# A fused delta-rule and feed-forward kernel whose opening stage is put in an order of its own: K loaded first, norms by a root on VectorE, weights decoded by three engines

## Chip, cores and metric

The kernel runs on one core of a Trainium2 chip. The metric is the time of one execution on the device in microseconds (us), as the median of several runs. The executions of the kernel before lie between 822 and 830 us over all chips used here.

## The reference, cut to what matters

```python
k_n = k / (np.linalg.norm(k, axis=-1, keepdims=True) + 1e-06)       # (4, 8, 768, 48)
for t in range(S):                                                 # S = 768
    y[:, :, t] = np.einsum('bhd,bhde->bhe', q[:, :, t], state)
    v_old = np.einsum('bhde,bhd->bhe', state, k_n[:, :, t])
    state = state + b[t] * outer(k_n[:, :, t], v[:, :, t] - v_old)
x = y.transpose(0, 2, 1, 3).reshape(3072, 384)
h = x @ w_in                                                       # 384 x 2048
out = (0.5 * h * (1 + erf(h / sqrt(2)))) @ w_out                   # 2048 x 384
```

The weights `w_in` and `w_out` arrive as float64. The kernel takes the 64 bits as two 32-bit words and builds float32 values from them; this is the "decode".

## The kernel before

The sequence is cut into 12 chunks of 64 steps. For two chunks together (a "group") a 32x32 triangular system per head is inverted on VectorE by sixty dependent operations (the "elimination"), carried over to the other half by small matmuls (the "joins"), and then each chunk has its state steps. The feed-forward of chunk c runs beside the state steps of chunk c+1. A scheduler arranges the instructions of each engine by the priorities that the program text gives.

The decode of one tile of 512 (w_in) or 384 (w_out) columns, where `hi` and `lo` are the two words, each with a stride of two:

```python
nc.vector.tensor_scalar(e, hi, 20, 0x7FF, op0=ALU.logical_shift_right, op1=ALU.bitwise_and)
nc.vector.tensor_scalar(bits, hi, 0xFFFFF, 0x100000, op0=ALU.bitwise_and, op1=ALU.bitwise_or)
nc.gpsimd.tensor_scalar(e, e, 1151.0, 896.0, op0=ALU.min, op1=ALU.max)
nc.gpsimd.tensor_scalar(e, e, -896.0, float(2 ** 23), op0=ALU.add, op1=ALU.mult)
nc.vector.scalar_tensor_tensor(e, hi, 0x80000000, e, ALU.bitwise_and, ALU.bitwise_or)
nc.vector.scalar_tensor_tensor(dst, lo, 2.0 ** -32, bits, ALU.mult, ALU.add)
nc.vector.scalar_tensor_tensor(dst, dst, 2.0 ** -20, e.bitcast(F32), ALU.mult, ALU.mult)
```

And the order of the opening:

```python
interleave(gram_steps(0) + gram_steps(1) + v_steps(0) + inverse_steps(0),
           [(1.0, decode, n) for n in range(6)])
interleave(state_steps(0), gram_steps(2) + v_steps(1), [(1.0, decode, n) for n in range(6, n_in)])
for c in range(1, NC):
    ...   # c == 1: state(1), gram(3), inverse(1), feed-forward 0 and the rest of the decodes
```

Of the kernel before, what the change touches and what calls it, by code (L numbers as in the profile page):

```python
# [8 lines left out]
F32 = mybir.dt.float32  # L9
# [7 lines left out]
def kernel(  # L17
# [68 lines left out]
    def fetch_in(dst, src, u):  # L86
        rows = slice(u.c * C, (u.c + 1) * C)
        for p in range(2):
            nc.sync.dma_start(out=dst[HALF[p]],  # L89
                              in_=src[2 * u.a + p, :, rows, :].rearrange("h t d -> t h d"))  # L90

    def load(c):
        if c >= NC:
            return
        for a in range(NA):
            u = tiles[c, a] = Unit()
            u.c, u.a, u.n = c, a, c * NA + a
            u.t = (c % 2) * NA + a
            u.Kp, u.Qp = Kp[u.n % NKS], Qp[u.n % NQS]
            fetch_in(u.Kp[:, :, 0:D], k, u)  # L100
            fetch_in(u.Qp[:, :, 0:D], q, u)
# [8 lines left out]
    w_out_sb = cpool.tile([128, NF, DM], F32)  # L110
    bt = w_in_sb[0:B * H, 0, 0:2 * S].rearrange("n (c p t) -> n c p t", p=2, t=C)
# [3 lines left out]
    load(0)  # L115
    load(1)
# [3 lines left out]
    make_identity(nc, ident)  # L120
    mask = cpool.tile([128, C], F32)
    nc.gpsimd.memset(mask, 1.0)
    for p in range(2):
        nc.gpsimd.affine_select(out=mask[HALF[p]], in_=mask[HALF[p]], compare_op=ALU.is_ge,
                                fill=0.0, base=-1, pattern=[[1, C]], channel_multiplier=-1)
# [3 lines left out]
    for i in range(NKS):  # L129
        nc.gpsimd.memset(Kp[i][:, :, D:], 0.0)  # L130
    St = cpool.tile([128, NA, 2, NP, D], F32)
    nc.vector.memset(St, 0.0)
    low = cpool.tile([128, HB, HB], F32)
    nc.gpsimd.memset(low, 1.0)
    nc.gpsimd.affine_select(out=low, in_=low, compare_op=ALU.is_ge, fill=0.0, base=-1,
                            pattern=[[1, HB], [-1, HB]], channel_multiplier=0)
    Zf = [cpool.tile([128, NU, C], F32, name=f"Zf{i}") for i in range(2)]
    for i in range(2):
        nc.gpsimd.memset(Zf[i], 0.0)
# [3 lines left out]
    psB = sq("psB", NC, B * H)  # L143
    for c in range(NC):
        nc.tensor.transpose(psB[:, c, :], bt[:, c].rearrange("n p t -> n (p t)"),
                            ident[0:B * H, 0:B * H])
    for p in range(2):
        src = psB[HALF[p]].rearrange("q c (a p h) -> q c a p h", p=2, h=H)[:, :, :, p, :]
        nc.vector.tensor_scalar_mul(beta_m[HALF[p]], src, -1.0)
# [3 lines left out]
    w_parts = [(w_in_sb[:, m, f:f + WC], moe_w_in[m * 128:(m + 1) * 128, f:f + WC])  # L153
               for f in range(0, DF, WC) for m in range(NM)]
    w_parts += [(w_out_sb[:, f, :], moe_w_out[f * 128:(f + 1) * 128, :]) for f in range(NF)]
    w_raw = {}
    n_in = len(w_parts) - NF
# [3 lines left out]
    NS = NF * DM // (2 * WC)  # L161

    def fetch(n):
        if n >= len(w_parts):
            return
        src = w_parts[n][1]
        if n < n_in:
            w_raw[n] = stage[:, n % NS]
        else:
            w_raw[n] = su.tile([128, DM, 2], U32, tag="w_raw", name="w_raw")  # L170
        nc.sync.dma_start(out=w_raw[n].rearrange("q n w -> q (n w)"), in_=src.bitcast(U32))

    def decode(n):

        if n >= n_in - 1:
            fetch(n + 1)
        dst = w_parts[n][0]
        bits = dst.bitcast(U32)
        w = dst.shape[1]
        raw = w_raw.pop(n)  # L180
        lo, hi = raw[:, :, 0], raw[:, :, 1]
        e = su.tile([128, WC], U32, tag="w_e", name="w_e")[:, 0:w]
        nc.vector.tensor_scalar(e, hi, 20, 0x7FF, op0=ALU.logical_shift_right,  # L183
                                op1=ALU.bitwise_and)
        nc.vector.tensor_scalar(bits, hi, 0xFFFFF, 0x100000, op0=ALU.bitwise_and,
                                op1=ALU.bitwise_or)
        nc.gpsimd.tensor_scalar(e, e, 1151.0, 896.0, op0=ALU.min, op1=ALU.max)  # L187
        nc.gpsimd.tensor_scalar(e, e, -896.0, float(2 ** 23), op0=ALU.add, op1=ALU.mult)
        nc.vector.scalar_tensor_tensor(e, hi, 0x80000000, e, ALU.bitwise_and, ALU.bitwise_or)  # L189
        nc.vector.scalar_tensor_tensor(dst, lo, 2.0 ** -32, bits, ALU.mult, ALU.add)  # L190
        nc.vector.scalar_tensor_tensor(dst, dst, 2.0 ** -20, e.bitcast(F32), ALU.mult, ALU.mult)
        if n + NS < n_in:
            fetch(n + NS)

# [7 lines left out]

    def prep(c):
        us = [tiles[c, a] for a in range(NA)]
        g = c // 2
        if c % 2 == 0:
            gms[g] = wk.tile([128, 2 * NA, H], F32, tag="gm", name="gm")
        gm = gms[g][:, us[0].t:us[0].t + NA]
        n = ns[c] = wk.tile([128, NA, H], F32, tag="n", name="n", bufs=4)
        for u in us:  # L210
            kd = u.Kp[:, :, 0:D]
            ksq = wk.tile([128, H, D], F32, tag="ksq", name="ksq")
            nc.gpsimd.tensor_tensor(ksq, kd, kd, op=ALU.mult)  # L213
            nc.vector.tensor_reduce(n[:, u.a], ksq, axis=AX.X, op=ALU.add)  # L214
        flat = n.rearrange("q a h -> q (a h)")
        nc.gpsimd.tensor_tensor(flat, flat, half, op=ALU.pow)
        nc.vector.tensor_scalar_add(n, n, 1e-6)
        r = wk.tile([128, NA, H], F32, tag="r", name="r")
        nc.vector.reciprocal(r, n)
        nc.vector.tensor_tensor(gm, beta_m[:, c], r, op=ALU.mult)  # L220
        nc.vector.tensor_tensor(gm, gm, r, op=ALU.mult)
        if c == 0:
            nc.vector.tensor_scalar_mul(g_p, gm, -1.0)
# [5 lines left out]
    def transposed(u):  # L229
        u.KQt = wk.tile([128, NP, 2, 2, C], F32, tag="KQt", name="KQt", bufs=6)  # L230
        for x, src in ((0, u.Kp), (1, u.Qp)):
            psT = sq("psT", NP, 128)
            flat = src.rearrange("q h d -> q (h d)")
            for j in range(NP):
                nc.tensor.transpose(psT[:, j, :], flat[:, j * 128:(j + 1) * 128], ident)  # L235
            nc.scalar.copy(u.KQt[:, :, :, x, :], psT.rearrange("q j (p n) -> q j p n", p=2))  # L236

    def grams(u):
        g = u.c // 2
        if u.t == 0:  # L240
            Ds[g] = wk.tile([128, NU, HB], F32, tag="diag", name="diag", bufs=1)
            Os[g] = wk.tile([128, NU, HB], F32, tag="off", name="off", bufs=1)
        u.P = wk.tile([128, H, C], F32, tag="P", name="P", bufs=6)
# [7 lines left out]
        G = wk.tile([128, NP, 2, 2 * C], F32, tag="G", name="G", bufs=1)  # L251
        for r in range(2):
            nc.scalar.copy(G[:, :, r, :], psG[:, r])  # L253
        G = G.rearrange("q j r n -> q (j r) n")
        span = slice(u.t * H, (u.t + 1) * H)
        nc.scalar.copy(Ds[g][:, span], G[:, :, 0:HB])
        for p in range(2):
            lower = slice(p * C + HB, (p + 1) * C)
            nc.scalar.copy(Ds[g][lower, span], G[lower, :, HB:C])
        nc.vector.tensor_tensor(Os[g][:, span], G[:, :, HB:C],  # L260
                                gms[g][:, u.t].unsqueeze(2).to_broadcast([128, H, HB]),
                                op=ALU.mult)
        nc.gpsimd.tensor_tensor(u.P, G[:, :, C:], mask_h, op=ALU.mult)  # L263

    def eliminate_steps(g):
        steps = []

        def flip():
            Nus[g] = wk.tile([128, HB, HB], F32, tag="Nu", name="Nu", bufs=1)
# [4 lines left out]
                                    op=ALU.mult)  # L274
            nc.vector.transpose(Nus[g], Ds[g].rearrange("q u n -> q n u"))
            nc.vector.tensor_tensor(Nus[g], Nus[g], gl, op=ALU.mult)
# [26 lines left out]
        steps = [(3.0, flip)]  # L303
# [31 lines left out]
    def gram_steps(c):  # L335
# [3 lines left out]
        return [(1.0, prep, c)] + [(1.0, fn, u) for fn in (transposed, grams) for u in us]  # L339
# [129 lines left out]
    def ffn_steps(c):  # L469
        steps = [(1.3, fc1, c, f) for f in range(NF)]  # L470
        return steps + [(2.7, fc2, tiles[c, a], f, f + 4)
                        for a in range(NA) for f in range(0, NF, 4)]
# [12 lines left out]

    load_v(0)
    for n in range(NS):
        fetch(n)
    interleave(gram_steps(0) + gram_steps(1) + v_steps(0) + inverse_steps(0),
               [(1.0, decode, n) for n in range(6)])  # L490
    load(2)
    load_v(1)
    interleave(state_steps(0), gram_steps(2) + v_steps(1), [(1.0, decode, n) for n in range(6, n_in)])
    for c in range(1, NC):
# [3 lines left out]
        more = gram_steps(c + 2) + v_steps(c + 1) + (inverse_steps(c // 2 + 1) if c % 2 else [])  # L498
        if c == 1:
            interleave(state_steps(c), more, ffn_steps(c - 1),  # L500
                       [(1.0, decode, n) for n in range(n_in, NW)] + [(1.4 * NF, None)])
            start.close()
        else:
            interleave(state_steps(c), more, ffn_steps(c - 1))
# [31 lines left out]
```

## Time and profile before

| | before |
|---|---|
| time, median of the runs beside the change | 826.2 us (823.5 to 829.0) |
| profiled execution | 825.5 us |
| first feed-forward matmul (chunk 0) | 126.5 us |
| second feed-forward (chunk 1) | 213.1 us |
| third feed-forward (chunk 2) | 267.6 us |
| TensorE busy after 213 us | 598.6 of 612 us |

From the second feed-forward on, TensorE has no room, so the time is decided by when the feed-forwards can start. The starts come from the timeline of TensorE (the 1st and 97th matmul into psH).

### The profile page before, as it was taken

How to read it: one execution, taken by the hardware profiler on the slowest of the kernel's cores; microseconds unless marked ns; L12 is line 12 of the kernel's file. 1: busy time of each engine (PE TensorE's matmuls, PEld its weight loads, DVE VectorE, ACT ScalarE, POOL GpSimd, SP SyncE). 2: the span in 40 equal slices, each digit the busy share in tenths (PEclk: the TensorE clock that was granted, in tenths of full speed). 3: DMA queues.
4: the chain of work that ended last, by engine and by line, in shares of the span. 5: the costliest groups of instructions: out<-in, count | busy, mean ns of one | idle time of the engine just before them, and what ended most of it. 6: DMA issues, size and time to landing. Idle time of an engine off the chain costs nothing.

```text
span 825.5 us, 18581 instructions
## 1 busy us (share of the span) xinstructions
PE 707.5 (86%) x8148; PEld 515.3 (62%) x8148; DVE 376.1 (46%) x874; ACT 220.4 (27%) x510; POOL 190.9 (23%) x178
## 2 busy tenths in 40 slices
PE   4111078967999999999989999989999999999997
PEld 4100066735776865866857867757768668677684
DVE  3597997896012594031791023971125931202000
ACT  4200054201331512332403324213325122021120
POOL 8735357413002303013202014012023000000000
PEclk8555558887899999999999999999999999999999
DMA  7266034401101201203101102011011000000000
GB/s 173 111 154 107 19 90 106 102 33 30 35 16 29 50 1 30 40 12 61 19 20 31 30 21 54 6 30 31 2 30 30 2 21 2 10 11 1 20 1 19
DMA packets 84784, 32.85 MB, mean 40 GB/s; under 512 B 78048, under 2 KB 81120, under 8 KB 84704
## 3 DMA queue, kind: packets, MB, share of 16 engines
q1 hardware_dynamic: 80064, 26.75, 14.7%
q10 hardware_dynamic: 4640, 4.92, 2.4%
q8 instruction: 64, 1.05, 0.5%
q14 instruction: 16, 0.13, 0.0%
HBM read 26.94 MB, written 4.72 MB: 38 GB/s over the span
## 4 chain that ended last, share of the span: by engine, by line
PE 67%; DVE 20%; POOL 5%; issue 3%; SPq 2%; ACT 1%; DMA 1%; POOLq 0%; DVEq 0%
PE psO L460 28%; PE psH L451 25%; DVE tmp L283 4%; DVE Nu L285 4%; POOL w_e L187 2%; DVE w_e L189 2%; PE psT L235 2%; PE psS L426 2%; PE psG L248 2%; SPq L89 2%; PE psK L365 2%; PE psJ L320 1%; PE psJ L323 1%; DVE U L391 1%; PE psU L385 1%
## 5 line engine op out<-in xcount | busy, mean ns | idle before, releaser
L451 PE MATMUL psH<-xT,w_in_sb 128*128 128x256 f32 x1152 | 273.8, 390 | 4.0 <-ACT g L454 3.3
L460 PE MATMUL psO<-w_out_sb,g 128*128 128x384 f32 x768 | 273.6, 506 | 0.0
L451 PEld LDWEIGHTS psH<-xT,w_in_sb 128*128 128x128 f32 x1152 | 214.6, 192 | 36.4 <-ACT g L454 3.7
L460 PEld LDWEIGHTS psO<-w_out_sb,g 128*128 128x128 f32 x768 | 143.8, 194 | 91.0 <-issue 7.3
L454 ACT ACTIVATE g<-psH 128x256 f32<-128x256 f32 x192 | 73.7, 384 | 180.5 <-PE psH L451 179.9
L391 DVE TENSOR_TENSOR U<-psU,gm 64x192 f32<-64x192 f32 x88 | 31.2, 354 | 108.4 <-PE psU L385 107.5
L283 DVE TENSOR_TENSOR tmp<-Nu 128x30 f32<-128x30 f32 (+9 forms) x180 | 63.2, 351 | 4.6
L285 DVE TENSOR_TENSOR Nu<-Nu,tmp 128x30 f32<-128x30 f32 (+9 forms) x180 | 63.3, 352 | 4.4
L263 POOL TENSOR_TENSOR P<-G,mask 128x512 f32<-128x512 f32 x24 | 35.4, 1477 | 103.9 <-ACT G L253 103.9
L464 ACT COPY o_sb<-psO 128x384 f32<-128x384 f32 x24 | 11.5, 479 | 152.4 <-PE psO L460 152.4
L320 PE MATMUL psJ<-XM,off 32*32 32x32 f32 x768 | 16.4, 203 | 40.3 <-DVE XM L294 40.3
L235 PE MATMUL psT<-ident,Kp 128*128 128x128 f32 x96 | 17.0, 307 | 39.1 <-DMA Kp<-in_k_dram 29.1
L418 DVE TENSOR_TENSOR x<-psY,y 64x192 f32<-64x192 f32 x88 | 31.0, 352 | 38.4 <-PE psY L410 24.4
L320 PEld LDWEIGHTS psJ<-XM,off 32*32 32x32 f32 x768 | 15.2, 119 | 46.7 <-issue 43.4
L301 POOL MEMSET Zf<- 32x1024 f32 x12 | 11.4, 954 | 140.4 <-DVE Zf L298 140.1
L213 POOL TENSOR_TENSOR ksq<-Kp 128x384 f32<-128x384 f32 x24 | 20.7, 864 | 90.3 <-DMA Kp<-in_k_dram 90.0
L375 DVE TENSOR_TENSOR W<-psK,V 128x384 f32<-128x384 f32 x22 | 12.3, 557 | 61.9 <-PE psK L365 61.6
L187 POOL TENSOR_SCALAR w_e<-w_e 128x384 uint32<-128x384 uint32 (+1 forms) x28 | 27.4, 977 | 55.2 <-DVE w_e L183 54.9
L329 ACT COPY XM<-psJ 32x512 f32<-32x512 f32 x24 | 13.9, 578 | 97.7 <-PE psJ L320 97.6
L235 PEld LDWEIGHTS psT<-ident,Kp 128*128 128x128 f32 x96 | 12.7, 157 | 41.9 <-issue 35.9
L236 ACT COPY KQt<-psT 128x512 f32<-128x512 f32 x48 | 26.7, 588 | 43.6 <-PE psT L235 39.5
L214 DVE TENSOR_REDUCE n<-ksq 128x8 f32<-128x384 f32 x24 | 13.2, 552 | 55.2 <-POOL ksq L213 55.2
(75 smaller groups left out, 669.9 us busy)
## 6 DMA issues: line engine op xcount, KB each, us to landing
w_out_sb<-in_moe_w_in_dram SPq DMA_DIRECT2D x12, 512.0 KB, 4.7
w_raw<-in_moe_w_out_dram SPq DMA_DIRECT2D x16, 384.0 KB, 3.3
Kp<-in_k_dram SPq DMA_DIRECT2D x48, 96.0 KB, 2.9
Qp<-in_q_dram SPq DMA_DIRECT2D x48, 96.0 KB, 3.0
V<-in_v_dram SPq DMA_DIRECT2D x48, 96.0 KB, 2.9
out_dram<-o_sb ACTq DMA_DIRECT2D x48, 96.0 KB, 2.2
w_in_sb<-in_beta_dram ACTq DMA_DIRECT2D x2, 96.0 KB, 3.4
```

The source lines that it names most:

```text
L187: nc.gpsimd.tensor_scalar(e, e, 1151.0, 896.0, op0=ALU.min, op1=ALU.max)
L235: nc.tensor.transpose(psT[:, j, :], flat[:, j * 128:(j + 1) * 128], ident)
L236: nc.scalar.copy(u.KQt[:, :, :, x, :], psT.rearrange("q j (p n) -> q j p n", p=2))
L263: nc.gpsimd.tensor_tensor(u.P, G[:, :, C:], mask_h, op=ALU.mult)
L283: nc.vector.tensor_tensor(tmp, nu[:, j + 1:, j:j + 1].to_broadcast([128, n, j]), nu[:, j:j + 1, 0:j].to_broadcast([128, n, j]), op=ALU.mult)
L285: nc.vector.tensor_tensor(nu[:, j + 1:, 0:j], nu[:, j + 1:, 0:j], tmp, op=ALU.add)
L320: nc.tensor.matmul(psJ[low, 0, col], lhsT=off[top, u, :], rhs=xm[top, u, :], start=True, stop=True)
L391: nc.vector.tensor_tensor(pairs(u.U[HALF[p]], s), pairs(psU[HALF[p ^ s], p], s), pairs(gv[HALF[p]], s), op=ALU.mult)
L418: nc.vector.tensor_tensor(dst, src, pairs(u.y[HALF[p ^ s]], s), op=ALU.add)
L451: nc.tensor.matmul(psH, lhsT=w_in_sb[:, m, f * 128:(f + 1) * 128], rhs=xTs[c][:, m, :], start=(m == 0), stop=(m == NM - 1))
L454: nc.scalar.activation(gs[f], psH, ACT.Gelu)
L460: nc.tensor.matmul(u.psO, lhsT=gs[f][:, u.a * 128:(u.a + 1) * 128], rhs=w_out_sb[:, f, :], start=(f == 0), stop=(f == NF - 1))
```

## The change

Its intent: do nothing in the opening but what the first feed-forward needs, and decode the weights beside that feed-forward, with the work split over VectorE, ScalarE and GpSimd. The diff, cut to its core:

```diff
+    for u in first:                                    # K of four units first, halves on two queues
+        fetch_in(u.Kp[:, :, 0:D], k, u, (nc.sync, nc.scalar))
     ...                                                # then beta on the ScalarE queue, then Q
+    cuts = [0, WC // 2] + list(range(WC, DF + 1, WC))  # first 512 columns of w_in as two 256s
@@ decode
-        nc.gpsimd.tensor_scalar(e, e, 1151.0, 896.0, op0=ALU.min, op1=ALU.max)
-        nc.gpsimd.tensor_scalar(e, e, -896.0, float(2 ** 23), op0=ALU.add, op1=ALU.mult)
+        nc.scalar.activation(e, e, ACT.Relu, bias=lim[:, 0:1], scale=-1.0)
+        nc.scalar.activation(e, e, ACT.Relu, bias=lim[:, 1:2], scale=-float(2 ** 23))
+        nc.gpsimd.tensor_scalar(lo.bitcast(F32), lo, 2.0 ** -52, None, op0=ALU.mult)
+        nc.scalar.mul(dst, bits, 2.0 ** -20)
+        nc.gpsimd.tensor_tensor(dst, dst, lo.bitcast(F32), op=ALU.add)
+    def signed(n):                                     # one tile later
         nc.vector.scalar_tensor_tensor(e, hi, 0x80000000, e, ALU.bitwise_and, ALU.bitwise_or)
-        nc.vector.scalar_tensor_tensor(dst, lo, 2.0 ** -32, bits, ALU.mult, ALU.add)
-        nc.vector.scalar_tensor_tensor(dst, dst, 2.0 ** -20, e.bitcast(F32), ALU.mult, ALU.mult)
+        nc.gpsimd.tensor_tensor(dst, dst, e.bitcast(F32), op=ALU.mult)
@@ order
+    by_hand.enter_context(tc.manual_schedule(engines={DVE, Pool, Activation, PE}))
     ...   # squares; transposes, beta, products; root on VectorE; pack; flip; split
+    for step in steps:                                 # the elimination, nothing beside it
+        if step[1] not in (join, None): step[1](*step[2:])
+    for _, fn, n in decode_steps(0, NM): fn(n)         # three 256-column tiles
     ...   # joins of chunk 0; V scaling
+    interleave(state_steps(0), decode_steps(NM, 2 * NM))
     ...   # joins of chunk 1
+    by_hand.close()
+    early = gram_steps(2) + v_steps(1) + state_steps(1) + gram_steps(3) + v_steps(2)
+    late = inverse_steps(1)
+    interleave(ffn_steps(0), [(s_[0] * scale, *s_[1:]) for s_ in early] + late,
+               codes + [(0.8 * sum(s_[0] for s_ in codes), None)])   # all other decodes
```

## The prediction

> **What bounds the kernel now.** I read the page first, then the table of busy time by stretch, then the timeline of VectorE and GpSimd in two short windows. From the page, the 40 slices (20.6 us each):
>
> ```profile
> PE   4111078967999999999989999989999999999997
> DVE  3597997896012594031791023971125931202000
> POOL 8735357413002303013202014012023000000000
> PEclk8555558887899999999999999999999999999999
> ```
>
> TensorE is busy without a break from slice 11 on. Before that it is nearly empty for 100 us and VectorE is full. So there are two regimes, and the change touches the first alone. The border is the first matmul of the second chunk's feed-forward, at 213 us (timeline of TensorE). The table by stretch, cut at the events I found in that timeline (flip of the first group 33, first join 102, first feed-forward matmul 126.5, last weight decoded 173.5, second feed-forward 213):
>
> ```profile
> core 0: us, PE busy (x) PEld busy (x) DVE busy (x) ACT busy (x) POOL busy (x), PEclk, DMA share, GB/s
> 0.00:33.00 33.00, 13.76 (x172) 11.14 (x172) 10.52 (x27) 14.81 (x29) 26.29 (x33) 0.74 0.64 161
> 33.00:102.00 69.00, 4.35 (x16) 2.86 (x16) 60.84 (x138) 2.34 (x4) 33.19 (x33) 0.50 0.41 91
> 102.00:126.50 24.50, 19.46 (x541) 17.48 (x541) 23.29 (x39) 12.66 (x29) 12.69 (x16) 0.50 0.36 93
> 126.50:173.50 47.00, 39.47 (x365) 29.64 (x362) 39.50 (x86) 14.79 (x35) 25.77 (x27) 0.90 0.37 97
> 173.50:213.00 39.50, 31.87 (x438) 20.66 (x438) 26.86 (x66) 5.28 (x10) 6.80 (x6) 0.75 0.08 17
> 213.00:825.00 612.00, 598.58 (x6629) 433.50 (x6622) 215.08 (x524) 170.54 (x404) 86.13 (x65) 0.99 0.11 22
> ```
>
> After 213 us TensorE is 98% busy: those 612 us stay whatever the opening does. What can be won lies in the first 213 us, of which the second row is the emptiest for TensorE: 69 us in which the elimination of the first group and the decoding of twelve input weight tiles and the first output tile share VectorE.
>
> VectorE and GpSimd both look partly free in that table, but in the timeline they hold each other up. VectorE first, then GpSimd, over the same microseconds:
>
> ```profile
> 139.60 1.42 DVE L185 TENSOR_SCALAR w_out_sb<-w_raw 128x384 uint32<-128x384 uint32 x1
> 143.17 1.62 DVE L189 SCALAR_TENSOR_TENSOR w_e<-w_raw,w_e 128x384 uint32<-128x384 uint32 x1 [0.41 <-POOL w_e L188]
> 144.82 0.56 DVE L191 SCALAR_TENSOR_TENSOR w_out_sb<-w_out_sb,w_e 128x384 f32<-128x384 f32 x1
> 145.30 0.35 DVE L183 TENSOR_SCALAR w_e<-w_raw 128x384 uint32<-128x384 uint32 x1
> ```
>
> ```profile
> 139.22 1.58 POOL L263 TENSOR_TENSOR P<-G,mask 128x512 f32<-128x512 f32 x1
> 143.11 1.27 POOL L263 TENSOR_TENSOR P<-G,mask 128x512 f32<-128x512 f32 x1
> ```
>
> An operation of 0.35 us took 1.42 and ended 0.2 us after GpSimd's; one of 0.56 took 1.62 and ended 0.4 us after. I laid the intervals of VectorE's tensor_scalar, scalar_tensor_tensor and SBUF-only tensor_tensor instructions and of GpSimd's operations that read SBUF over each other: one or the other runs in 127 of the 140 us from 33 to 173. The two engines together are one resource here, 91% full. That, not VectorE's own share, is the bound of the opening.
>
> **What the Trainium skill says.** "SBUF — State Buffer", section "Who interferes with whom": VectorE and GpSimd share one port pair as an exclusive lock; a VectorE instruction with two SBUF inputs, or in a two-port mode (tensor_scalar can be), blocks against GpSimd reads; ScalarE waits for nobody. The two fences agree (1.42 against 0.35 us). "GPSIMD Engine Reference", section "Elementwise — side-by-side cycle accounting": a two-input operation on GpSimd takes 1.96 times VectorE's time at 2048 elements. The trace has 0.83 us for 128x384 (V, L226) against VectorE's 0.55 for a two-input operation of that size (L191): 1.5 times. "ScalarE: Activation LUTs", section "Table sets: the hidden batching unit": relu and copy are in every set, so the new Relu beside Gelu should cost no table loads. The kernel before has two loads of 1.28 us, with copies beside Gelu; it has no Relu. "DMA: Bandwidth & Descriptors", section "Issuing engines are not separate DMA queues": a second queue saves issue time only. Before, each K or Q issue took SyncE 0.63 us, 16 of them 10.2 us, so issue time is what the first 12 us hang on.
>
> **The change part by part.** Durations are start to start where nothing waited, from the timeline and the groups by form.
>
> *Until the first flip (31.2 us before).* K goes first, on two queues; all four pairs of inputs should still land only by 11 to 13 us, since 16 loads run on the same DMA engines and each transpose pair waits for its Q too. Then four products, each 2.0 us at half clock, and the copies of G (0.59 us, no longer through one buffer, whose waits cost ACT 3.5 and 3.8 us). The pow on GpSimd (2.9 us, twice) becomes 11 small VectorE operations near 0.2 us, off this path. Last pack about 1 us. Flip at 19.5 us: 11.5 us earlier.
>
> *Elimination alone.* The sixty operations without a wait: fifteen sizes from 0.19 to 0.41 us sum to 4.97, four times each 19.9, with gaps near 0.03 some 21.7 us. Around it the flip (1.95+1.25) and three transposes back (2.0+1.8+1.8): 30.5 us. GpSimd now makes off and P of four units beside it (0.6+1.4 each, 8 us), which hold the same port: I add 6. End at 19.5+30.5+6 = 56 us, against 105.6.
>
> *To the first feed-forward.* Three quarter-megabyte tiles are decoded ahead of the joins' copies in ScalarE's order (4 us), a join of half a group is 2x1.9 at half clock plus copies 2x1.2 (6 us, part overlapped), the first state took 17.5 us before and should take 12 to 14 with less on VectorE, and the second pair of joins sits ahead of the feed-forward on TensorE (some of 5 us). 56+23 = 79 us, against 126.5. This is the visible gain: 47 us.
>
> *What is given back.* By 126.5 the kernel before had decoded 17 of 28 tiles; the new one has three full-tile equivalents by 79. Left are nine of 512 columns and sixteen of 384. Per tile of 512: VectorE 0.34+0.34+0.60 = 1.28; GpSimd one tensor_scalar 0.70 and two two-input operations of 1.07 (0.79 for 384, scaled) = 2.84; together 4.1 us of the port (before: VectorE 2.5, GpSimd 1.25, 3.75). Per tile of 384: 1.01+2.17 = 3.2 (before 2.9). ScalarE takes three operations of 0.5 to 0.6, about 40 us in all, where it is free. So **the decode is taken off VectorE but not off the port**: 9x4.1+16x3.2 = 88 us. Beside it two chunks' gram work (P 4x1.47, pow 2x2.9, ksq 4x0.82, off and norms 3: 18 us) and V scaling (3.3): 109 us. My sums of single durations overstate the occupied time: for before up to 213 us the same bookkeeping gives 183 where the overlaid intervals give 166, so 0.91. Decoding is then over at the earliest at 79+0.91x109 = 178 us. The second group's elimination (25 us of port, 23 scaled) is ranked in the later half but fills gaps: between nothing and all of it comes ahead, 178 to 201. I take half, 189, and 1 to 3 us for the last matmuls: second feed-forward at 190 to 191.
>
> TensorE is not the bound in that stretch: the first feed-forward is 96x0.22+64x0.32 = 42 us plus about 23 for grams, state and joins, 65 us of 110.
>
> *Sum.* 190.5 + (823.6 - 213) = 801 us; 802 is recorded.
>
> **The rivals.** (a) *The port takes everything back*: the scheduler puts the second group's joins ahead of the second feed-forward in TensorE's order, and they wait until the whole elimination is through. All port work then ends near 201, transposes back and joins add 8 to 12: second feed-forward at 209 to 213, total 820 to 824. For it: before, TensorE waited 7.6 us for U and 4.3 for XM in this way. Against: the wait for XM was short, and there are 41 us of feed-forward to fill in. (b) *The port is not what it seems*: with GpSimd's operations long and VectorE's few, and ScalarE in between, VectorE's PSUM work and stream transposes (3x1.9 us a group) overlap GpSimd and the port is fully used; decoding ends near 170, total near 780. Against: 91% was used already. (c) *The opening hides TensorE's clock*: with TensorE 60% busy from 79 on it may stay at half clock (0.50 in the second and third rows), and 65 us become 100, near the decode's length; 5 to 10 us worse.
>
> **Range and chances.** Between (b) and (a) with (c): 780 to 826, 802 in the middle; 8 in 10 within 782 to 822. The 2% border is 807, so a second feed-forward later than 196 makes it "same". The half taken of the elimination decides it: faster 0.62, same 0.35, slower 0.03. Slower needs the decode past 225 us, which only a bad order of instructions would do.
>
> **What would show it.** In the new profile: the first flip near 19 and back-transposes ended near 56; first feed-forward matmul near 79; last output tile finished near 180 to 195; second feed-forward near 190, and 611 us from there to the end. GpSimd's busy time up from 191 to over 240, VectorE's down by 30 to 45, ScalarE's up by about 45, still two table loads. VectorE's scalar_tensor_tensor in the decode should show means well above 0.55 for 384 columns, ended by GpSimd. Wrong: if the decoding ends by 165 the port was not the limit; if TensorE waits more than 10 us at the joins of the second group it is rival (a); if the first feed-forward starts after 95, the hand-set order stalls and my chain there is wrong.

## The result, and the profile after

The change is slower: 857.6 us (855.6 to 859.1) against 826.2, ratio 1.038 with a 95% interval of 1.033 to 1.043. My range ended at 822.

| | before | predicted | after |
|---|---|---|---|
| first flip of the elimination | 31.2 | 19.5 | 27.6 |
| elimination and its transposes over | 105.6 | 56 | 72.8 |
| first feed-forward | 126.5 | 79 | 105.0 |
| last weight tile decoded | 175.3 | 189 | 219.6 |
| second feed-forward | 213.1 | 190.5 | 225.9 |
| third feed-forward | 267.6 | (245) | 299.4 |
| profiled end | 825.5 | 802 | 853.8 |

From the third feed-forward on the two are alike (558 us before, 554 after). Everything that was lost was lost earlier: 13 us until the second feed-forward and 19 between the second and the third. In all sixteen kernels it takes 554 to 560 us from the third feed-forward to the end, but 612 to 634 from the second. So the start of the third feed-forward, not of the second, tells the time. The page's slices of the kernel after (21.3 us each):

```profile
PE   4101565658779999999999999999999989999998
DVE  4486457767941259402297122693033960201100
POOL 2925988799111140301501202303014000000000
PEclk9655576788859999999999999999999999999999
```

GpSimd (POOL) is now the busiest engine of slices 5 to 10, mostly with eights and nines. Busy time by stretch, in the columns of the prediction's table (PE, PEld, DVE, ACT, POOL, clock, DMA):

```profile
0.00:27.60 27.60, 13.55 (x172) 11.11 (x172) 12.08 (x37) 10.15 (x18) 11.59 (x29) 1.00 0.91 168
27.60:72.60 45.00, 1.92 (x64) 1.82 (x64) 31.87 (x72) 0.00 (x0) 18.60 (x16) 0.50 0.25 51
72.60:105.00 32.40, 12.92 (x330) 11.39 (x331) 13.99 (x34) 16.09 (x38) 29.73 (x30) 0.50 0.34 97
105.00:220.00 115.00, 75.42 (x707) 51.84 (x707) 80.35 (x122) 61.99 (x127) 96.68 (x79) 0.77 0.31 79
```

In the third and fourth rows GpSimd is busy 92% and 84% of the time. The overlay of the prediction (VectorE's port operations and GpSimd's, laid over each other) gives 110 of the 115 us of the fourth row. The pair is the bound, as predicted, and holds on longer than predicted. The waits of 104 to 226 us, longest in total, times, longest single one, say the same from VectorE's side: it waits to take a new exponent buffer (there are two) until GpSimd's last product has freed the old one.

```profile
DVE w_e L188 <- POOL w_in_sb L202: 12.9, 8, 5.0
DVE w_e L188 <- POOL w_out_sb L202: 11.2, 11, 3.3
```

What one tile costs GpSimd, from the groups by form. First the kernel before (its two limit operations, and the V scaling from which I had taken the price of a two-input operation):

```profile
L226 POOL TENSOR_TENSOR V<-V,n 128x384 f32<-128x384 f32 x24 | 20.7, 863 | 68.4 <-DMA V<-in_v_dram 56.9 <-PE psT L235 4.0 <-PE psH L451 3.9
L188 POOL TENSOR_SCALAR w_e<-w_e 128x384 uint32<-128x384 uint32 x16 | 10.1, 629 | 1.2
```

and the kernel after, the low word, the sum and the last product:

```profile
L194 POOL TENSOR_SCALAR w_raw<-w_raw 128x384 f32<-128x384 uint32 x8 | 11.0, 1370 | 0.7
L196 POOL TENSOR_TENSOR w_out_sb<-w_out_sb,w_raw 128x384 f32<-128x384 f32 x8 | 9.3, 1165 | 0.2
L202 POOL TENSOR_TENSOR w_out_sb<-w_out_sb,w_e 128x384 f32<-128x384 f32 x16 | 16.1, 1005 | 9.4 <-DVE w_e L201 8.0 <-DVE tmp L336 0.8
```

The means contain blocking by VectorE. The fastest of each form contain none: 1.20 us for the low word at 384 columns, where I had reckoned with 0.59 start to start (0.51 was the fastest of before), and 0.99 to 1.00 for each two-input operation, where I had 0.79. At 512 columns they are 1.53 and 1.27, where I had 0.70 and 1.07.

The hand-set stretch has its own delays. In VectorE's timeline after (start, duration, what; in brackets the idle time ahead of it and what ended it):

```profile
29.57 1.93 DVE L329 TENSOR_TENSOR Nu<-Nu,XM 128x1024 f32<-128x1024 f32 x1
39.88 0.55 DVE L236 TENSOR_REDUCE n<-ksq 128x8 f32<-128x384 f32 x1 [8.38 <-POOL ksq L235]
49.87 0.79 DVE L226 TENSOR_SCALAR n<-n 128x16 f32<-128x16 f32 x1 [2.82 <-POOL n L247]
```

The flip's product ends at 31.5 us, and the elimination could go on. But the next instruction in VectorE's order is the sum of squares of the third chunk. The text puts it long after; it is outside the hand-set region, and the scheduler has slipped it in. It waits for GpSimd, which at that time makes P and off and, also slipped in, four low words of output weights. VectorE stands idle 8.4 us, and 2.8 us more for the root of the same chunk. Further on, TensorE's timeline after:

```profile
69.43 1.92 PE L373 MATMUL psJ<-XM,off 32*32 32x32 f32 x64 [44.54 <-DVE XM L347]
82.00 0.31 PE L376 MATMUL psJ<-Zf,XM 32*32 32x32 f32 x2 [10.65 <-ACT XM L382]
104.96 1.06 PE L504 MATMUL psH<-xT,w_in_sb 128*128 128x256 f32 x2
225.88 7.50 PE L504 MATMUL psH<-xT,w_in_sb 128*128 128x256 f32 x34
240.38 3.62 PE L373 MATMUL psJ<-XM,off 32*32 32x32 f32 x128 [7.00 <-DVE XM L347]
245.94 3.62 PE L376 MATMUL psJ<-Zf,XM 32*32 32x32 f32 x128
```

Between 69 and 82 us the joins wait for copies that stand behind the first decodes in ScalarE's order. And after the second feed-forward has begun at 225.9, the joins of the second group come only at 240.4, after 7.0 us of waiting. In the kernel before they came at 196 to 213, ahead of the second feed-forward. From the second to the third feed-forward it takes 54.5 us before and 73.5 after. The rows of that stretch, before and after, in the columns of above:

```profile
213.10:267.60 54.50, 54.50 (x577) 39.65 (x575) 9.86 (x24) 16.91 (x40) 7.92 (x7) 1.00 0.15 30
225.90:299.40 73.50, 66.50 (x824) 49.28 (x822) 26.60 (x62) 19.80 (x45) 9.85 (x9) 0.84 0.10 20
```

Of these 19 us, 7.0 are this wait and 7.2 are the joins themselves, work that only changed places. Most of the rest lies in the same 96 matmuls into psH, which take 27.0 us for 22.5: the granted clock is 0.84 in this stretch for 1.00 before, and 0.50 from 240.4 to 250, right after the wait.

### The profile page after: what moved, and what is told of

Its sections match the earlier page's. It is cut to its first block, busy times and chain, and to the rows that moved or that the text cites. A ratio compares the mean times of both kernels' runs of the same rounds, so it can differ in the third digit from the quotient of the medians.

```text
span 853.8 us, 18720 instructions
## 1 busy us (share of the span) xinstructions
PE 717.0 (84%) x8148; PEld 520.8 (61%) x8148; DVE 375.3 (44%) x839; ACT 262.2 (31%) x592; POOL 244.7 (29%) x219
## 3 DMA queue, kind: packets, MB, share of 16 engines
q8 instruction: 64, 1.05, 0.5%
## 4 chain that ended last, share of the span: by engine, by line
PE 53%; DVE 19%; POOL 4%; issue 3%; ACT 3%; POOLq 0%; DVEq 0%; ACTq 0%
PE psO L513 23%; PE psH L504 19%; DVE Nu L338 6%; DVE tmp L336 6%; DVE U L444 2%; PE psT L274 2%; PE psJ L373 2%; PE psJ L376 1%; PE psS L479 1%; PE psK L418 1%; POOL w_out_sb L202 1%; DVE Nu L328 1%; PE psG L282 1%; DVE w_e L188 1%; ACT G L289 1%
## 5 line engine op out<-in xcount | busy, mean ns | idle before, releaser
L504 PE MATMUL psH<-xT,w_in_sb 128*128 128x256 f32 x1152 | 286.2, 400 | 9.6 <-ACT g L507 8.9
L513 PE MATMUL psO<-w_out_sb,g 128*128 128x384 f32 x768 | 270.1, 502 | 10.7 <-ACT g L507 5.6
L504 PEld LDWEIGHTS psH<-xT,w_in_sb 128*128 128x128 f32 x1152 | 219.1, 197 | 45.0 <-ACT g L507 10.7
L444 DVE TENSOR_TENSOR U<-psU,gm 64x192 f32<-64x192 f32 x88 | 31.2, 354 | 107.4 <-PE psU L438 106.4
L354 POOL MEMSET Zf<- 32x1024 f32 x12 | 11.9, 990 | 172.5 <-DVE Zf L351 150.9
L309 POOL TENSOR_TENSOR P<-G,mask 128x512 f32<-128x512 f32 x22 | 32.1, 1459 | 99.6 <-ACT G L289 99.6
L190 ACT ACTIVATE w_e<-w_e,lim 128x384 uint32<-128x384 uint32 (+2 forms) x31 | 19.5, 629 | 92.6 <-DVE w_e L188 92.5
L235 POOL TENSOR_TENSOR ksq<-Kp 128x384 f32<-128x384 f32 x22 | 18.3, 832 | 69.7 <-DMA Kp<-in_k_dram 69.2
L264 POOL TENSOR_TENSOR V<-V,n 128x384 f32<-128x384 f32 x24 | 20.7, 867 | 60.6 <-DMA V<-in_v_dram 53.2
L428 DVE TENSOR_TENSOR W<-psK,V 128x384 f32<-128x384 f32 x22 | 12.2, 555 | 57.4 <-PE psK L418 57.4
L289 ACT COPY G<-psG 128x512 f32<-128x512 f32 x44 | 23.8, 589 | 37.2 <-PE psG L282 27.4
L247 POOL TENSOR_TENSOR n<-n,half 128x16 f32<-128x16 f32 x10 | 29.2, 2918 | 9.5 <-DVE n L236 9.5
```

Of the source, the lines that this page charges most:

```text
L247: nc.gpsimd.tensor_tensor(flat, flat, half, op=ALU.pow)
L264: nc.gpsimd.tensor_tensor(u.V, u.V, ns[u.c][:, u.a].unsqueeze(2).to_broadcast([128, H, D]), op=ALU.mult)
L289: copy(G[:, :, r, :], psG[:, r])
L309: nc.gpsimd.tensor_tensor(u.P, u.G[:, :, C:], mask_h, op=ALU.mult)
L444: nc.vector.tensor_tensor(pairs(u.U[HALF[p]], s), pairs(psU[HALF[p ^ s], p], s), pairs(gv[HALF[p]], s), op=ALU.mult)
L504: nc.tensor.matmul(psH, lhsT=w_in_sb[:, m, f * 128:(f + 1) * 128], rhs=xTs[c][:, m, :], start=(m == 0), stop=(m == NM - 1))
```

## The experiments

Two theories stood at first. **A**: the three-engine decode puts more work on GpSimd than the port that it shares with VectorE can carry. **B**: the hand-set order is what costs (the slipped-in work, the joins behind the decodes, the late first feed-forward). Fourteen kernels ran, thirteen of them timed in three rounds.

### e1: the change's order with the arithmetic of before

```diff
-        (the two Relu, the three GpSimd operations and ScalarE's mul)
+        (the two limit operations on GpSimd, the sum and the last product on VectorE, as before)
```

> The changed kernel's order of work, but each weight tile decoded with the arithmetic of before (five operations on VectorE, two short ones on GpSimd, none on ScalarE). Theory A, the three-engine decode makes GpSimd the bound (3.25 us of it per 384-column tile and 4.2 per 512-column tile instead of 1.0 and 1.3): the second feed-forward starts 20 us earlier, near 205 instead of 226, and the total is 830 to 840. Theory B, the hand-set order is what costs (automatic work slipped into the elimination, joins behind the decode, first feed-forward at 105 instead of the 79 I predicted): the total stays within 8 us of 857.

Measured: 811.6 us, ratio 0.984 (0.979 to 0.989) to before. First feed-forward at 89.7, second at 183.2. It beats even what theory A had said. With the old arithmetic the new order is an improvement of 1.6%, and theory B falls as the main cause.

### e2: the kernel before with the three-engine arithmetic

> The kernel before with its own order of work, but with the three-engine arithmetic of the change for every tile. Theory A: GpSimd gets 28 tiles of 3 to 4 us in place of 1 to 1.3, some 60 us more in the first 213; VectorE gets 30 us less; the total rises to 845 to 860. Theory B: within 8 us of 826.

Measured: 838.1 us, ratio 1.013 (1.009 to 1.018). The direction is A's, the size is not: 12 us, not 20 to 34. The same arithmetic costs 46 us in the new order (857.6 against 811.6). In the old order decoding starts at 33 us beside the elimination and has 167 us to end in; in the new order most of it starts after 72 us. The two parts of the change are worse together than apart: the order leaves less time for the decode, and the arithmetic makes it longer. Read the other way, theory B is not nothing: with the three-engine arithmetic the second feed-forward starts at the same time in either order (225.3 in e2, 225.9 in the change), and the 19.5 us between e2 and the change lie between the second and the third (54.5 and 73.5). In e1 that stretch is long too, 70.0; there an earlier second feed-forward pays for it.

### e3 and e4: taking GpSimd's operations away, one and then two

```diff
e3:
-        nc.gpsimd.tensor_scalar(lo.bitcast(F32), lo, 2.0 ** -52, None, op0=ALU.mult)
+        nc.scalar.mul(lo.bitcast(F32), lo, 2.0 ** -52)
e4 (the factor 2^-20 goes into the exponent's limit, 235 for 255):
-        (low word on GpSimd, mul on ScalarE, sum on GpSimd)
+        nc.vector.scalar_tensor_tensor(dst, lo, 2.0 ** -32, bits, ALU.mult, ALU.add)
```

> The changed kernel with one operation moved: the scaling of the low word (1.2 us per 384 columns, 1.65 per 512 on GpSimd, strided in and out) goes to ScalarE. Theory A: 25 tiles times about 1.3 us, 34 us, leave GpSimd in the stretch from 105 to 220 us; ScalarE is only 54% busy there; the decode ends near 190 to 195 and the total is 828 to 838. Theory B: gain of 8 us or less.

> The changed kernel with the low word added to the mantissa by one VectorE operation as in the kernel before, the power of two put in the exponent's limit: GpSimd keeps only the last product (1.0 us per 384 columns), VectorE has four operations instead of three. Theory A: 60 us leave GpSimd and 13 come to VectorE; the decode is bound by nothing long, the first feed-forward starts near 98, the second near 190, total 815 to 825. Theory B: gain of 8 us or less.

Measured: 840.7 us for e3 (1.018), 821.7 us for e4 (0.995). e4 lies in the range of A; e3 gained 17 us where A had said at least 19. The time goes down with each operation that leaves GpSimd.

### e5 and e6: the hand-set order mended

The loads that feed the slipped-in work are held back by tiny writes on VectorE after the elimination, so the work cannot come earlier; the joins and the V scaling go ahead of the decodes.

```diff
-    (fetch of output weights, load(2), load_v(1))
     for step in steps: ...                      # the elimination
+    for s in slots: nc.vector.memset(s[:, 0:1, :], 0)
+    for i in range(4, 6): nc.vector.memset(Kp[i][:, :, 0:1], 0.0)
+    (fetch of output weights, load(2), load_v(1))
+    (V scaling, joins of chunk 0)
     for _, fn, n in decode_steps(0, NM): fn(n)
-    (joins of chunk 0, V scaling)
```

> The change with its three-engine arithmetic, its hand-set stretch mended in two places: the loads that feed automatic work (inputs of the third chunk, first output weights) are held until the first elimination is over, and the first joins and V scalings stand ahead of the first three decodes. If the hand-set stretch is a cost of its own: the elimination runs without the 11 us of waits for GpSimd's squares and powers and ends near 56 instead of 67, the first feed-forward starts near 82 to 88 instead of 105, and the total falls by 10 to 20 us, to 838 to 848. If GpSimd's decode work is the only bound after that, what is won at the start is waited for again at the second feed-forward (still near 218 to 226) and the total stays above 850.

> The same two mendings with the decode arithmetic of before. With GpSimd relieved, the earlier start should pass through: first feed-forward near 78, second near 172 to 176 instead of 183, total 800 to 806. If VectorE with GpSimd on the shared port is the bound of the whole opening (as my prediction had it), the total stays at 808 to 813.

Measured: e5 (three engines) 855.1 us, e6 (old arithmetic) 808.4 us, ratio 0.976 (0.973 to 0.979) to before. In e5 the mending of the elimination worked; VectorE's timeline of e5, the flip's product and the first transpose back:

```profile
29.52 1.92 DVE L329 TENSOR_TENSOR Nu<-Nu,XM 128x1024 f32<-128x1024 f32 x1
57.17 1.98 DVE L347 STREAM_TRANSPOSE XM<-Nu 128x1024 f32<-128x1024 f32 x1
```

The sixty operations now take 25.6 us without a wait, and the transposes back end 10 us earlier than in the change. Yet the first feed-forward starts only 6 us earlier (98.9) and the second only 3 (222.6), and in the time 2 to 3 us are left. With the old arithmetic it is the same: first feed-forward 3.6 us earlier, total 3.2 (by the ratios, which allow for the chips, the mending is worth 0.5% in e5 and 0.8% in e6). So the delays of the hand-set order are real but hidden: what they delay has to wait for the decode anyhow. I had expected more of e6 (800 to 806); my words for "the port is the bound of the whole opening" were 808 to 813, and that came.

### e7 and e8: the second group's elimination earlier

```diff
-    interleave(ffn_steps(0), [early, scaled] + late, codes + ...)
+    interleave(ffn_steps(0), v_steps(1) + state_steps(1) + v_steps(2),
+               gram_steps(2) + gram_steps(3) + inverse_steps(1), codes + ...)
```

> The change's order with the arithmetic of before, and the second group's grams and elimination ranked across the whole first feed-forward and not in its second half. Theory: the 70 us from the second to the third feed-forward (54.5 in the kernel before) come from the late second elimination (joins wait until 208). With it earlier the third feed-forward starts near 240 to 246 instead of 253 and the total is 798 to 806. If the port is full, the decode is pushed back by as much: total 809 to 815, the second feed-forward near 198.

> Both mendings and the earlier second group, with the arithmetic of before. If the gains of the two add up: 790 to 800. If one bound serves both: no better than the better of the two runs before it, within 3 us.

Measured: e7 823.0 us, e8 820.9 us, worse than e1 and e6 by 11 to 13. The elimination started earlier (141 for 180 us) but ended only 4 us earlier (202.0 for 206.3), the decode ended 8 us later, and the second feed-forward went from 183 to 196. The pair of engines was full, as my second branch said, though the loss was larger than I had put there (823 for 809 to 815), and e8 fits neither of its branches. Nor did the stretch from the second to the third feed-forward shrink (69.6 us in e7 for 70.0), for the elimination still ended (202.0) after the second feed-forward had begun (196.4) and the joins still fell between the two; the wait for it went from 5.2 to 3.3 us. So what an elimination in time would bring is not shown. A late second elimination is the smaller evil.

### e9, e10 and e12: the pair relieved

The exponent's limits stay on ScalarE as in the change, and all the rest of the decode is on VectorE, so GpSimd has no part in it. As in e4, the factor 2^-20 goes into the limit.

```diff
-        (low word, sum and last product on GpSimd, mul on ScalarE)
+        nc.vector.scalar_tensor_tensor(dst, lo, 2.0 ** -32, bits, ALU.mult, ALU.add)
+        nc.vector.tensor_tensor(dst, dst, e.bitcast(F32), op=ALU.mult)     # in signed()
```

> The mended order of the 808 us run, with the exponent's limits on ScalarE (two Relu, as in the change) and the rest of the decode on VectorE (five operations, 1.9 us per 384 columns and 2.5 per 512); GpSimd has no part in the decode. Theory, the pair of VectorE and GpSimd that shares one port is the bound of the opening: 1.0 to 1.25 us per tile, about 25 us in all over 25 tiles, leave the pair; the second feed-forward starts at 160 to 170 instead of 181 and the total is 788 to 799. If VectorE alone is the bound: 804 to 810. If ScalarE's latency between two VectorE operations makes waits: worse than 810.

> The kernel before with its own order, only the exponent's two limit operations moved from GpSimd to ScalarE. Theory of the shared port: 28 us leave the pair, of which the part that blocked VectorE or was waited for comes back; total 808 to 818. If VectorE's own work is the bound: 824 to 832.

> The 795 us run with the second group's grams and elimination ranked across the whole first feed-forward. In the 795 us run the third feed-forward starts 69 us after the second (54.5 in the kernel before) because the second elimination ends at 187. If the pair of VectorE and GpSimd has room now that the limits are on ScalarE: second feed-forward near 172, third near 228, total 785 to 791. If the pair is still full, the decode gives way as it did with the arithmetic of before (823 against 812): total 800 to 808.

Measured: e9, in the mended order, 794.7 us, ratio 0.964 (0.960 to 0.969). e10, the kernel before with the limits moved, 806.7 us, ratio 0.978 (0.974 to 0.982). e9 lies in the range of the shared port, e10 came 1.3 us below it (808 to 818). e10 is not quite a single alteration: the sum now stands ahead of the sign operation, which gives the limits more time, and the last product is a plain one. Of the 20.3 us by which its second feed-forward is earlier (192.8), some 7 are shorter waits of VectorE for the limits (10.4 us before, 3.5 in e10). The rest fits the shorter VectorE operations; the sign operation, in the kernel before and in e10:

```profile
L189 DVE SCALAR_TENSOR_TENSOR w_e<-w_raw,w_e 128x384 uint32<-128x384 uint32 x16 | 11.4, 715 | 5.0 <-POOL w_e L188 5.0
L193 DVE SCALAR_TENSOR_TENSOR w_e<-w_raw,w_e 128x384 uint32<-128x384 uint32 x16 | 9.2, 574 | 3.7 <-ACT w_e L189 3.5
```

From e6 to e9 the comparison is cleaner: VectorE keeps five operations to a tile, its waits for the limits are alike (2.1 and 1.8 us), and the second feed-forward goes from 181.2 to 165.9. That speaks for the pair against VectorE alone; e3, e4 and e14 by themselves would fit GpSimd alone as the bound of the change (84% busy). e9 beats both kernels by more than 2% and is the best. Its stretch from the first to the second feed-forward:

```profile
83.00:166.00 83.00, 69.62 (x733) 48.29 (x730) 74.43 (x164) 55.63 (x110) 35.13 (x15) 0.89 0.49 119
```

83 us for the same 25 tiles, where the change took 121 (105 to 226). The overlay gives some 74 us for the pair, still 90%. e12, with the second group earlier as in e7, 800.3 us: the pair has no room yet.

### e11, e13 and e14: why GpSimd's scaling is long

The low word's scaling took 1.20 us where the limits of before took 0.51. Three things differ: the stride, the output type (float for unsigned), and one arithmetic step in place of two.

```diff
e11:
-        nc.gpsimd.tensor_scalar(lo.bitcast(F32), lo, 2.0 ** -52, None, op0=ALU.mult)
-        nc.scalar.mul(dst, bits, 2.0 ** -20)
+        nc.scalar.mul(lo.bitcast(F32), lo, 2.0 ** -52)
+        nc.gpsimd.tensor_scalar(dst, bits, 2.0 ** -20, None, op0=ALU.mult)
e13 = e11 and:
+        nc.gpsimd.tensor_scalar(dst, bits, 2.0 ** -20, 1.0, op0=ALU.mult, op1=ALU.mult)
e14 = the change and:
+        nc.gpsimd.tensor_scalar(lo.bitcast(F32), lo, 2.0 ** -52, 1.0, op0=ALU.mult, op1=ALU.mult)
```

> The change with two operations exchanged: GpSimd scales the mantissa (contiguous unsigned to float, in place), ScalarE scales the low word (strided in and out). GpSimd keeps as many operations as in the change. If the stride made GpSimd's scaling long (1.2 us per 384 columns): it falls to 0.5 to 0.65, 25 tiles save about 17 us of GpSimd, total 840 to 848. If the conversion from unsigned to float made it long: it stays at 1.2 and the total at 853 to 862.

> The swapped run with one thing more: GpSimd's scaling of the mantissa (contiguous, unsigned to float) is given two arithmetic steps, as the kernel before's limit operations had (unsigned to unsigned, 0.51 us at best for 384 columns). If the output type makes it long, it stays at 1.17 to 1.3 us. If the form with a single arithmetic step is the slow one, it falls to 0.5 to 0.65.

> The change as it is, but GpSimd's scaling of the low word written with two arithmetic steps (times 2 to the -52, times 1). If the single-step form alone made it long: 1.20 falls to 0.51 to 0.65 us per 384 columns although it is strided, 25 tiles give about 18 us of GpSimd back, and the total is 838 to 848. If the stride costs as well: it stays above 0.9 and the total above 850.

e11 took 858.6 us, and the contiguous operation was as long as the strided one. The groups by form of e11:

```profile
L195 POOL TENSOR_SCALAR w_out_sb<-w_out_sb 128x384 f32<-128x384 uint32 x16 | 21.0, 1312 | 3.2 <-DVE w_out_sb L192 2.1
```

So the stride is not it, and I took it for the type conversion. e13, one look of state unknown at 846.9 us, has the same operands and two steps:

```profile
L195 POOL TENSOR_SCALAR w_out_sb<-w_out_sb 128x384 f32<-128x384 uint32 x16 | 10.3, 644 | 3.6 <-DVE w_out_sb L192 2.7
```

The conversion is not it either. It is **the form with a single arithmetic step**: multiplying by 1 as a second step halves the duration (fastest 0.51 us). e14 puts that into the change itself, strided operands and all:

```profile
L194 POOL TENSOR_SCALAR w_raw<-w_raw 128x384 f32<-128x384 uint32 x8 | 4.5, 566 | 0.7
```

1.37 us on average become 0.57, and the time falls to 844.1 us, ratio 1.023 (1.019 to 1.027) to before. One literal in the program was worth 13 us.

### The row as a whole

GpSimd's share of the decode against the time, all in the change's order, unmended; GpSimd's column adds the median durations per tile of 384 columns:

| kernel | GpSimd per tile, us | VectorE operations | second feed-forward | time |
|---|---|---|---|---|
| the change | 3.2 | 3 | 225.9 | 857.6 |
| e14, low word in two steps | 2.6 | 3 | 213.7 | 844.1 |
| e3, low word on ScalarE | 2.0 | 3 | 208.8 | 840.7 |
| e4, only the last product | 1.0 | 4 | 189.7 | 821.7 |
| e1, arithmetic of before | 1.2 | 5 | 183.2 | 811.6 |

e4 and e1 show that GpSimd's time is not all: e4 has less work on both engines of the pair and is slower. In e4 GpSimd waited 39.8 us for VectorE's sign operation between 93 and 190 us, in 23 waits; the tile's way through three engines is longer and only two exponent buffers exist. Why exactly e4 loses the 10 us I did not test; more exponent buffers would be the test.

## Why the prediction was wrong

The miss at the third feed-forward is 54 us (299.4 for 245): 35 until the second, 19 between the second and the third. They have different causes.

**The bound was named rightly.** The pair on one port was to carry the time of the decode; it was occupied 110 of 115 us in that stretch, and every experiment that relieved the pair (e1, e3, e4, e9, e10, e14) brought time, the one that filled it otherwise (e7) cost some. "Taken off VectorE but not off the port" is what happened.

**The step that failed is the price of a tile on GpSimd**: "one tensor_scalar 0.70 and two two-input operations of 1.07 (0.79 for 384, scaled) = 2.84", and 2.17 for 384 columns. In the trace the fastest are 1.53+1.27+1.26 = 4.1 us and 1.20+1.00+0.99 = 3.2. Over 12 tile equivalents of 512 and 16 of 384 that is about 31 us more for the pair. The overlay agrees: from the start to the second feed-forward the pair was occupied 191 us. By my terms it should have been some 158: 166 as before, plus 8 for the dearer tiles (0.91 times 12x0.35+16x0.3), less half of the second elimination (11) and two powers (5). This difference of 33 us is nearly all of the 35 by which the second feed-forward came late. That is bookkeeping and not an experiment: e14 takes about 21 us out of GpSimd's low words (0.68, 0.89 and 0.45 us for 384, 512 and 256 columns), and the second feed-forward starts 12.2 us earlier (213.7). So 12 of the 35 us are shown for the single-step form; the share of the two-input operations is argued. Two causes:

- The one-input term I took from an operation of another form. That its single-step form runs at less than half the speed was not visible in the kernel before, which has no such operation on GpSimd. e11, e13 and e14 found it, 13 us of the result.
- The two-input term I took from V's scaling, whose second operand is one value repeated along each head (0.82 us at best at 384 columns). With two full operands it is 0.99. The page that I cited for it, "GPSIMD Engine Reference", section "Elementwise — side-by-side cycle accounting", has 4497 ns at 2048 elements, 2.2 ns for an element; from 384 to 512 columns the trace has (1.26-0.99)/128 = 2.1 ns. The slope agrees, but scaled down to 384 columns the page's figure is 0.84 us and would not have warned me. Its ratio of 1.96 would have, applied to VectorE's 0.55 (1.08 us), and this I set aside for V's row. The kernel before had a fitting row too, P from G and the mask at 512 columns, 1.26 us at best.

**The first feed-forward at 79 us** was wrong by 26 us, and my own sign for that (a start after 95) came true. The trace shows three places: the flip 8.1 us late, since TensorE waited 6.8 us for Q, whose second half stood on ScalarE's queue behind beta, and VectorE's root stood behind beta too; the elimination with its transposes 8.7 us longer (45.2 for 36.5), with 11 us of waits for slipped-in work; and the way from there to the feed-forward 9.2 us longer (32.2 for 23), with joins 11 us behind the decodes. (The terms of this last part add up to 27 to 29 us; I had taken 23 for overlap that I did not work out.) Along the chain of the prediction these 26 us are most of the 35, for from the first feed-forward to the last weight it took 115 us where I had 110; there the dearer tiles were offset by an elimination that came after the decode and not half before it (flip at 207), and by work that had slipped ahead. But e5 and e6 showed that mending the last two moved the end by 2 to 3 us. The reason was sound as to where the gain is seen, and wrong in that it is a gain: it was not the first but the second feed-forward that mattered, and this was tied to the sum of the pair's work. The first delay, Q behind beta, no run took away.

**"611 us from there to the end"** is the second step that failed: 628 in the profile. I had named this as rival (a), joins of the second group that wait, and gave as a test a wait of over 10 us. The wait was 7.0 us, and the joins' own 7.2 us moved behind the border. In that sense the border I had chosen was not clean: what stands between two feed-forwards can change sides. From the third feed-forward on it would have been. For the same reason "Slower needs the decode past 225 us" was wrong: the last weight was ready at 219.6. What lengthens this stretch is read from the trace (the wait, the joins, the clock); no run took it away.

**Right:** VectorE pays in the elimination what I had reckoned, where nothing disturbs it (25.6 us in e5 with 8 us of GpSimd beside it, for the 21.7+6 of the prediction); Relu beside Gelu costs no table loads (two before, two after); ScalarE's busy time rose by 42 us (about 45 predicted), GpSimd's to 245 us (over 240). VectorE's was to fall by 30 to 45 and fell by 0.8 only: what its operations lost in number the remaining ones gained in length, as in L188 at 384 columns with means of 0.86 and 1.05 us for 0.37 before (L183). I had looked for this in scalar_tensor_tensor, where it is small (L201, 0.63 and 0.68 us for 0.55). Two small misreadings had no weight: the last weight before ends at 175.3 and not at 173.5, and the sixteen K and Q issues take SyncE from 0.8 to 11.9 us, 11.1 and not 10.2.

Rival (c), TensorE's clock, stays open: it was 0.77 from 105 to 220 us, and 0.84 between the second and third feed-forward, but no run tells what a full clock there would have saved.

## What to carry to other kernels

When work is moved between two engines that block each other, add up the time of the pair and not of the engine that is relieved; here moving two of VectorE's operations to GpSimd made the pair's sum larger, and moving two of GpSimd's to ScalarE, with hardly anything else, made it smaller and won 18 us in the old order. Price each added operation from a row with the same form, the same number of full operands and the same steps, and where the kernel has none, measure it before anything is built on it. An earlier start of a stage is worth something only as far as the resource that ends the stage is freed too.

## What the Trainium skill lacked or had wrong

- "GPSIMD Engine Reference", section "Engine selection", calls one-input operations on GpSimd roughly line-rate. For tensor_scalar with a single arithmetic step the runs show 1.20 us at best for 128x384 (1.53 for 512), and 0.51 with a second step that multiplies by 1 (0.53 with strided operands). No page that I read has this.
- The same page, "Elementwise — side-by-side cycle accounting", gives one figure for two-input operations. Its 2.2 ns for an element agree with the slope for two full operands (2.1 ns between 0.99 us for 384 columns and 1.26 for 512), but scaled down it is too short at these sizes (0.84 and 1.12). With the second operand repeated within each head, or with the same tile as both operands, it was 0.82.
- "SBUF — State Buffer", section "Who interferes with whom", is borne out (a tensor_scalar of VectorE at 384 columns, 0.35 us at best, took 0.86 and 1.05 on average beside GpSimd's decode, with one of the two running in 110 of 115 us); what it lacks is the sum: that two engines under this lock are to be budgeted as one. VectorE's busy time, 376 us before and 375 after with three operations to a tile for five, hides it, since the waiting counts as busy.
- "ScalarE: Activation LUTs", section "Rules for kernel authors", advises VectorE and not ScalarE for relu, max and min. It leaves out the case in which VectorE and GpSimd are full together: the two limits as Relu on ScalarE and not as min and max on GpSimd (0.61 us each at 384 columns) took the kernel before from 824.5 to 806.7 us. No run had them on VectorE.
